# Ten of 25 score blocks: one float32 product a head becomes two float32r products of stacked parts

## The chip, the cores and the metric

The kernel runs on one core of a Trainium2 chip. TensorE (PE in the profile, its weight loads PEld) multiplies, VectorE (DVE), ScalarE (ACT) and GpSimd (POOL) do the elementwise work, and SyncE (SP) issues the DMAs. The metric is the device time of one execution in microseconds (us), as the median of several runs.

## What is computed

A chunked linear recurrence (state-space attention) over 4 batches, 8 heads and 768 steps feeds one layer with a gate. Cut to what matters:

```python
for c in range(nc):                       # chunks of the sequence
    cum = np.cumsum(log_a[chunk])
    L = causal * np.exp(cum[i] - cum[j])
    CB = np.einsum('bhin,bhjn->bhij', Cc, Bc)      # n = 16: this product is changed
    y = einsum(CB * L, xc) + einsum(Cc, state) * np.exp(cum)
    state = decay * state + einsum(Bc * decay_from_j, xc)
h = y @ w_in                              # 3072 x 256 by 256 x 2048
out = (h - tanh(h)) @ w_out               # 2048 x 256
```

All inputs are float32 (the weights arrive as 64-bit floats and are converted in the kernel). Only the product C B^T, with a contraction of 16, is touched.

## The kernel before

The sequence of each batch is cut into 7 chunks of 112 steps (the last has 96): 28 chunks in 14 groups of two. In SBUF each chunk has 128 rows, 16 for the state and 112 for its steps, so that C B^T and C times the state are one product. The eight heads lie as four row groups of 32 partitions (index `i`, 16 of the 32 partitions used) with two heads each (index `w`).

- `load_bc` brings B and C of a group (tile `bc`, three buffers) with four DMAs, one to each row group. `prep` lets POOL write the identity into the state's columns.
- `differences` makes the decay's exponents in bfloat16 (tile `att`, L510). `inner` makes C B^T into the same PSUM tile (L519): for each of 8 heads a float32 product of 16 x 128 weights by up to 116 columns, 16 matmul instructions on PE for the 8 products. `att` has one buffer.
- `weigh` turns `att` into `lt`: exp on ACT (L534), product on DVE (L538), causal mask on POOL (L541). `chunk_y` multiplies `lt` by x (L567) and updates the state (L573). From chunk 10 on, one PE step issues differences and inner of chunk k+1, and then y of chunk k. Such a step is called a chunk block here.
- The layer runs in float32r, a float32 rounded to fewer bits that PE takes in one instruction: operands are split into a high and a low part and three products are summed. `mm1` makes `ph` (L644, 12 matmuls of 256 columns), ACT makes tanh (L659), DVE subtracts (L663, after which the `ph` buffer, one of two, is free), ACT rounds (`gh`, L667), DVE takes the rest (`gl`, L674), and `mm2` makes `o` (L706, 12 matmuls), two steps later. Its sums are taken out by DVE (`pt`, L721, L738) or by ACT and DVE (`ob`).

Each engine works through its own list in order. The lists come from a planner, `Order`: every operation has an engine, a cost that is written in the source and dependencies, and a table `RANK`, one number for each operation, sets the priority. The table was made anew for the change.

Of the kernel before, what the change touches and what calls it, by code (L numbers as in the profile page):

```python
# [9 lines left out]
F32 = mybir.dt.float32  # L10
# [38 lines left out]
MORE = 4  # L49

RANK = """
# [201 lines left out]
def tile_ssm_moe(ctx: ExitStack, tc: tile.TileContext, a, x, bn, bc, wts, out):  # L253
# [30 lines left out]
    def load_bc(G):  # L284


        d = grp[G]
        d["n_bc"] = slot("bc", NGB)

        def fn(i):  # L290
            if i == 0:
                d["bc"] = p2.tile([P, 2, CPG * (P + Q)], F32, tag="bc", name=f"bc{G}", bufs=NGB)
            nc.sync.dma_start(out=d["bc"][32 * i : 32 * i + N], in_=bc[G, i])  # L293

        for i in range(4):
            op("SP", 0.42, lambda i=i: fn(i), w=[d["n_bc"]], dma=KB // 2)
# [36 lines left out]
    cp.tile([P, P - AHEAD], F32, name="behind")  # L333
# [52 lines left out]
    def prep(G):  # L386
# [17 lines left out]
        op("POOL", 0.95, fn_b, r=["wdec", "bi", d["n_b"]], w=[d["n_bw"]])  # L404

# [97 lines left out]
    def need_a(ck):  # L503
        s = ck >= SPAN[0].stop
        return [grp[ck // CPG]["n_bc"], l_c[s], r_c[s]]
# [7 lines left out]
    def inner(ck, more=0):  # L513
        d, at = grp[ck // CPG], CPG * P + ck % CPG * Q
        bb, cc = operands(ck)[0], d["bc"][:, :, at - more : at + qlen(ck)]
        for w in range(2):
            for i in range(4):
                r = slice(32 * i, 32 * i + N)
                nc.tensor.matmul(out=place[1][:, i, 2 + w, N - more : N + qlen(ck)], lhsT=bb[r, w], rhs=cc[r, w],  # L519
                                 start=True, stop=True)  # L520
# [246 lines left out]
    par = cp.tile([P, 2], F32, name="par")  # L767
    ncf = cp.tile([P, N], F32, name="ncf")
# [34 lines left out]
    def consts_dve():  # L803
# [6 lines left out]
        nc.vector.tensor_scalar(out=idn, in0=ncf, scalar1=pidf[:, 1:2], scalar2=None, op0=ALU.is_equal)  # L810

# [26 lines left out]
    op("DVE", 0.9, consts_dve, r=["pid"], w=["idn", "par"])  # L838
# [83 lines left out]
    def plan(g, fn, *args):  # L922
        todo.setdefault(max(g, 0), []).append((fn, args))
# [11 lines left out]
    for ck in at_:  # L935
        if ck <= joint:
            plan(at_[ck][0], chunk_a, ck)
        plan(at_[ck][1], chunk_y, ck, ck >= joint and ck + 1 in at_)
        if (ck + 1) % CPG == 0 and ck // CPG + NGB < NG:
            plan(at_[ck][1], group, ck // CPG + NGB)  # L940
# [59 lines left out]
```

## Time and profile before

| | |
|---|---|
| median of 3 runs | 334.74 us (334.14, 334.74, 337.77) |
| profiled execution | 337.32 us, of which the span is 335.5 us |
| granted clock of TensorE, mean | 0.994 |
| PE, PEld busy | 97%, 93% of the span |
| DVE, ACT, POOL busy | 67%, 57%, 17% of the span |

The span runs from the first to the last instruction; 1.8 us of the profiled execution lie outside. Matmuls overlap on PE, so busy time is not proof of full use; distances from start to start say more. The last ten chunk blocks of the span, at 186.6 to 287 us, are those in which the product is changed.

### The profile page before, as it was taken

How to read it: one execution, taken by the hardware profiler on the slowest of the kernel's cores; microseconds unless marked ns; L12 is line 12 of the kernel's file. 1: busy time of each engine (PE TensorE's matmuls, PEld its weight loads, DVE VectorE, ACT ScalarE, POOL GpSimd, SP SyncE). 2: the span in 40 equal slices, each digit the busy share in tenths (PEclk: the TensorE clock that was granted, in tenths of full speed). 3: DMA queues.
4: the chain of work that ended last, by engine and by line, in shares of the span. 5: the costliest groups of instructions: out<-in, count | busy, mean ns of one | idle time of the engine just before them, and what ended most of it. 6: DMA issues, size and time to landing. Idle time of an engine off the chain costs nothing.

```text
span 335.5 us, 9070 instructions
## 1 busy us (share of the span) xinstructions
PE 325.0 (97%) x3860; PEld 312.8 (93%) x3860; DVE 225.5 (67%) x332; ACT 191.3 (57%) x404; POOL 55.9 (17%) x74
## 2 busy tenths in 40 slices
PE   7979999899999999999999999999999999999995
PEld 6767789899999999999999999999999999999995
DVE  2998999998899966544655655655655655654552
ACT  5866888766565634344655645643655645644441
POOL 6543563310021110000111101101111101100000
PEclk9998999999999999999999999999999999999999
DMA  6959756630011101200211200200200100000000
GB/s 183 243 148 300 230 157 154 202 133 2 3 45 31 47 23 43 64 2 0 63 48 31 64 14 17 64 9 24 63 3 3 33 2 2 31 2 2 31 2 32
DMA packets 12472, 21.41 MB, mean 64 GB/s; under 512 B 2848, under 2 KB 7648, under 8 KB 12432
## 3 DMA queue, kind: packets, MB, share of 16 engines
q1 hardware_dynamic: 12432, 20.84, 21.3%
q8 instruction: 30, 0.49, 0.6%
q14 instruction: 10, 0.08, 0.1%
HBM read 17.51 MB, written 3.32 MB: 62 GB/s over the span
## 4 chain that ended last, share of the span: by engine, by line
PE 86%; DMA 7%; SPq 3%; DVE 2%; issue 1%; POOL 1%; ACT 0%; DVEq 0%
PE o L706 38%; PE ph L644 37%; PE y L567 3%; PE att L519 3%; DMA x<-x_d 2%; DMA raw<-w_d 2%; DMA bc<-bc_d 2%; PE ph L628 2%; DMA braw<-bn_d 1%; SPq L293 1%; PE att L510 1%; PE y L573 1%; PE o L698 1%; POOL lt L541 1%; SPq L324 1%
## 5 line engine op out<-in xcount | busy, mean ns | idle before, releaser
L663 DVE TENSOR_TENSOR g<-ph,g 128x512 f32<-128x512 f32 x96 | 65.9, 690 | 57.9 <-ACT g L659 57.9
L659 ACT ACTIVATE g<-ph 128x512 f32<-128x512 f32 x96 | 57.2, 598 | 74.6 <-PE ph L644 71.4
L644 PE MATMUL ph<-xh,wh 128*128 128x256 f32 x376 | 95.5, 278 | 0.9 <-DVE g L663 0.9
L644 PE MATMUL ph<-xh,wl 128*128 128x256 f32 x376 | 94.9, 277 | 0.0
L674 DVE TENSOR_TENSOR gl<-g,gh 128x512 fp32r<-128x512 f32 x94 | 66.1, 706 | 26.6 <-ACT gh L667 24.2
L667 ACT CAST gh<-g 128x512 fp32r<-128x512 f32 x94 | 58.2, 619 | 36.9 <-DVE g L663 28.8
L644 PE MATMUL ph<-xl,wh 128*128 128x256 f32 x376 | 73.5, 277 | 0.0
L644 PEld LDWEIGHTS ph<-xh,wh 128*128 128x128 f32 x376 | 70.7, 188 | 1.3 <-DVE g L663 1.0
L644 PEld LDWEIGHTS ph<-xh,wl 128*128 128x128 f32 x376 | 70.6, 188 | 0.0
L706 PE MATMUL o<-gh,wh 128*128 128x256 f32 x376 | 60.5, 283 | 0.0
L706 PE MATMUL o<-gh,wl 128*128 128x256 f32 x376 | 58.1, 277 | 0.0
L706 PE MATMUL o<-gl,wh 128*128 128x256 f32 x376 | 58.1, 277 | 0.0
L644 PEld LDWEIGHTS ph<-xl,wh 128*128 128x128 f32 x376 | 56.8, 188 | 0.0
L541 POOL TENSOR_SCALAR_AFFINE_SELECT lt<-lt 128x896 f32<-128x896 f32 (+1 forms) x25 | 28.7, 1148 | 160.9 <-DVE lt L538 145.1
L706 PEld LDWEIGHTS o<-gh,wh 128*128 128x128 f32 x376 | 49.9, 188 | 1.1
L706 PEld LDWEIGHTS o<-gl,wh 128*128 128x128 f32 x376 | 49.8, 188 | 0.0
L706 PEld LDWEIGHTS o<-gh,wl 128*128 128x128 f32 x376 | 49.8, 188 | 0.0
L538 DVE TENSOR_TENSOR lt<-att,lt 128x896 f32<-128x896 f32 (+1 forms) x25 | 26.6, 1065 | 3.4 <-ACT lt L534 2.8
L534 ACT ACTIVATE lt<-att 128x896 f32<-128x896 f32 (+1 forms) x25 | 22.6, 903 | 1.9 <-PE att L519 0.7
L578 ACT COPY x<-y 16x64 f32<-16x64 f32 x96 | 19.4, 202 | 5.4 <-DVE xl L596 3.5
L394 POOL TENSOR_TENSOR bw<-braw,wdec 128x256 f32<-128x256 f32 x14 | 10.3, 746 | 58.2 <-PE y L573 54.4
L567 PE MATMUL y<-lt,x 128*32 128x112 f32 (+1 forms) x448 | 16.3, 263 | 3.1 <-ACT x L578 2.4
(79 smaller groups left out, 258.4 us busy)
## 6 DMA issues: line engine op xcount, KB each, us to landing
raw<-w_d SPq DMA_DIRECT2D x16, 512.0 KB
x<-x_d SPq DMA_DIRECT2D x14, 256.0 KB
bc<-bc_d SPq DMA_DIRECT2D x56, 60.0 KB
out_d<-ob SPq DMA_DIRECT2D x16, 128.0 KB
braw<-bn_d SPq DMA_DIRECT2D x14, 112.0 KB
out_d<-pt SPq DMA_DIRECT2D x8, 128.0 KB
cum<-parts SPq DMA_DIRECT2D x1, 168.0 KB
lt_c<-cum SPq DMA_DIRECT2D x4, 27.0 KB
```

What stands on the lines that cost most here:

```text
L394: nc.gpsimd.tensor_tensor(out=d["b"].rearrange("p c (h n) -> p c h n", h=H), in0=d["braw"].rearrange("p c (h n) -> p c h n", h=H), in1=wd. ...
L534: nc.scalar.activation(k["l"][:, :, 0:q].rearrange("p (i w) q -> p i w q", i=4), place[1][:, :, 0:2, N : N + q], AF.Exp)
L538: nc.vector.tensor_tensor(out=lt, in0=place[1][:, :, 2:4, N : N + q], in1=lt, op=ALU.mult)
L541: nc.gpsimd.affine_select(out=k["l"][:, :, 0:q], in_=k["l"][:, :, 0:q], pattern=[[0, H], [1, q]], compare_op=ALU.is_ge, fill=0.0, base=N, ...
L567: nc.tensor.matmul(out=y[D * h : D * h + D, hg * Q : hg * Q + q], lhsT=d["x"][:, cg, P * hg + D * h : P * hg + D * h + D], rhs=k["l"][:, 4 ...
L578: nc.scalar.copy(grp[(ck + 1) // CPG]["x"][0:N, (ck + 1) % CPG, 2 * D * i : 2 * D * i + 2 * D], k["y"][D * i : D * i + N, H * D : H * D + ...
L644: nc.tensor.matmul(out=ph[:, j, :], lhsT=w_[:, u, 0, k, j * P : (j + 1) * P], rhs=d[("xh", "xl")[p]][:, k, ts], start=p == 0 and k == 0 an ...
L659: nc.scalar.activation(g, gs[t, u][0], AF.Tanh)
L663: nc.vector.tensor_tensor(out=g, in0=ph, in1=g, op=ALU.subtract)
L667: nc.scalar.copy(gh, gs[t, u][1])
L674: on.tensor_tensor(out=gl, in0=g, in1=gh.bitcast(F32), op=ALU.subtract)
L706: nc.tensor.matmul(out=po[t, seg][:, e, :], lhsT=w_[:, u, 1, j, e * P : (e + 1) * P], rhs=g[:, j, :], start=u == seg[0] and k == 0 and j = ...
```

## The change

For groups 9 to 13 (chunks 18 to 27) C B^T is made from float32r parts. B is loaded twice, into both halves of each row group's 32 partitions, and a new step `part_bc` makes from it a tile `bs`: upper half minus the high part of B, lower half its low part, and beside it the high part of C with matching signs. One product with a contraction of 32 then gives high·high + low·high. A second tile, `b2`, holds the low part of C, and a product with a contraction of 16 adds high·low. So 8 float32 products become 16 float32r products, which accumulate in pairs.

```diff
+PARTED = 9
 def load_bc(G):
+    rows, src = (2 * N, bc2[G - PARTED]) if G >= PARTED else (N, bc[G])
-        nc.sync.dma_start(out=d["bc"][32 * i : 32 * i + N], in_=bc[G, i])
+        nc.sync.dma_start(out=d["bc"][32 * i : 32 * i + rows], in_=src[i])
-cp.tile([P, P - AHEAD], F32, name="behind")
+cp.tile([P, P - AHEAD - 40], F32, name="behind")
+def part_bc(G):
+    def fn_h():   # bs: bufs 2
+        nc.scalar.copy(d["bs"][:, :, bb], d["bc"][:, :, bb])
+    def fn_c():
+        nc.scalar.activation(d["bs"][:, :, cc], d["bc"][:, :, cc], AF.Copy, scale=sgn[:, 1:2])
+    def fn_l():
+        nc.vector.scalar_tensor_tensor(out=d["bs"][:, :, bb], in0=d["bc"][:, :, bb], scalar=sgn[:, 0:1],
+                                       in1=d["bs"][:, :, bb].bitcast(F32), op0=ALU.mult, op1=ALU.subtract)
+    def fn_2():
+        nc.vector.scalar_tensor_tensor(out=d["b2"], in0=d["bc"][:, :, wide], scalar=-1.0,
+                                       in1=d["bs"][:, :, wide].bitcast(F32), op0=ALU.mult, op1=ALU.subtract)
+    op("ACT", 0.62, fn_h, ...); op("ACT", 0.55, fn_c, ...); op("DVE", 0.7, fn_l, ...); op("DVE", 0.65, fn_2, ...)
 def inner(ck, more=0):
+    if "bs" in d:
+        for w in range(2):
+            for j in range(2):
+                for i in range(4):
+                    r = slice(32 * i, 32 * i + (2 - j) * N)
+                    rhs = b2[r, w] if j else d["bs"][r, w, at - more : at + qlen(ck)]
+                    nc.tensor.matmul(out=place[1][:, i, 2 + w, N - more : N + qlen(ck)],
+                                     lhsT=d["bs"][r, w, g * P : (g + 1) * P], rhs=rhs, start=j == 0, stop=j == 1)
+        return
...
+        if (ck + 1) % CPG == 0 and PARTED <= ck // CPG + 2 < NG:
+            plan(at_[ck][1], part_bc, ck // CPG + 2)
-    nc = bacc.Bacc("TRN2", target_bir_lowering=False, num_devices=1)
+    nc = bacc.Bacc("TRN2", target_bir_lowering=False, num_devices=1, dynamic_dma_scratch_size=1024)
```

Two small instructions on DVE at the start make the signs `sgn`. The costs that the planner has for PE are as before. The numbers in a tile's name below are those of its chunk or group (`bs9` is of group 9), or of sequence tile and step (`ph6_1`). `x4` are four products of the program.

PE, the chunk block of chunks 18 and 17, the first that is changed. Before:

```order
L644 MATMUL ph6_1_2717<-xl2_2427,wh_84 128x256 x2
L510 LDWEIGHTS lt_c_106
L510 MATMUL att_198<-rt_c_107,lt_c_106 128x2x112
L519 MATMUL att_198<-bc9_1650 128x116 x8
L567 MATMUL y17_2746<-lt17_2645,x8_1519 32x112 x8
```

And of the change, at the same place:

```order
L687 MATMUL ph6_1_2742<-xl2_2027,wh_84 128x256 x2
L543 LDWEIGHTS lt_c_107
L543 MATMUL att_201<-rt_c_108,lt_c_107 128x2x112
L555 MATMUL att_201<-bs9_1748 128x116 x4
L555 MATMUL att_201<-b29_1893,bs9_1748 128x116 x4
L555 MATMUL att_201<-bs9_1748 128x116 x4
L555 MATMUL att_201<-b29_1893,bs9_1748 128x116 x4
L610 MATMUL y17_2780<-lt17_2660,x8_1522 32x112 x8
```

The block stays between the same neighbours; only its middle changes. (The pair of rows for the weights and the matmul of `differences` stands four times in both and is shown once.) Elsewhere on PE one chunk block, of chunks 15 and 14, moves: it stood at 160 us of the profiled span, amid the sequence tile 5, and now stands ahead of `o0_6`, six pieces of the layer after the block at 111 us.

DVE, the busiest place that gets new work, just after the last weights are converted (`wl`, at 111 us before). Before:

```order
L370 TENSOR_TENSOR wl_85<-wv7_1348,wh_84 128x1024
L663 TENSOR_TENSOR g0_6_1745<-ph0_6_1677,g0_6_1745 128x512
L596 TENSOR_TENSOR xl1_806<-y13_1723,xh1_797 128x2x96
L674 TENSOR_TENSOR gl3_4_1782<-g3_4_1598,gh3_4_1671 128x512
L674 TENSOR_TENSOR gl3_5_1786<-g3_5_1692,gh3_5_1742 128x512
L674 TENSOR_TENSOR gl0_6_1803<-g0_6_1745,gh0_6_1784 128x512
L721 TENSOR_TENSOR pt2_986<-o2_4_1695,pt2_986 128x512
L663 TENSOR_TENSOR g0_7_1801<-ph0_7_1768,g0_7_1801 128x512
L538 TENSOR_TENSOR lt14_1765<-att_198,lt14_1765 128x896
```

And of the change:

```order
L373 TENSOR_TENSOR wl_85<-wv7_1351,wh_84 128x1024
L717 TENSOR_TENSOR gl3_4_1767<-g3_4_1601,gh3_4_1674 128x512
L717 TENSOR_TENSOR gl3_5_1771<-g3_5_1695,gh3_5_1745 128x512
L764 TENSOR_TENSOR pt2_989<-o2_4_1698,pt2_989 128x512
L639 TENSOR_TENSOR xl1_809<-y13_1726,xh1_800 128x2x96
L706 TENSOR_TENSOR g0_6_1789<-ph0_6_1680,g0_6_1789 128x512
L581 TENSOR_TENSOR lt14_1769<-att_201,lt14_1769 128x896
L706 TENSOR_TENSOR g0_7_1805<-ph0_7_1773,g0_7_1805 128x512
L717 TENSOR_TENSOR gl0_6_1826<-g0_6_1789,gh0_6_1809 128x512
L425 SCALAR_TENSOR_TENSOR bs9_1748<-bc9_1653,sgn_95,bs9_1748 128x2x256
```

`g0_6` moves behind two `gl`, a `pt` and `xl`, and the first of the new operations follows four rows later. 

SP, the loads of the last groups. Before, `bc10` follows the four stores of `pt`, and `bc11` to `bc13` come one by one, each beside its `x`. Of the change:

```order
L296 DMA bc10_1913<-bc2_d 32x960 x4
L791 DMA out_d<-pt0_568 128x256 x2
L791 DMA out_d<-pt1_906 128x256 x2
L791 DMA out_d<-pt2_989 128x256 x2
L791 DMA out_d<-pt3_1174 128x256 x2
L791 DMA out_d<-ob4_2426 128x256 x2
L308 DMA x10_2518<-x_d 128x512
L317 DMA braw1_101<-bn_d 112x256
L296 DMA bc11_2653<-bc2_d 32x960 x4
L296 DMA bc12_2678<-bc2_d 32x960 x4
L296 DMA bc13_2703<-bc2_d 32x960 x4
```

`bc10` now stands ahead of the stores, and the last three groups follow each other, each with twice the partitions (32 for 16).

More of the change, by code (lines that the diff above doesn't have):

```diff
@@ L252, in tile_ssm_moe @@
 @with_exitstack
-def tile_ssm_moe(ctx: ExitStack, tc: tile.TileContext, a, x, bn, bc, wts, out):
+def tile_ssm_moe(ctx: ExitStack, tc: tile.TileContext, a, x, bn, bc, bc2, wts, out):
     nc = tc.nc
@@ L292, in fn @@
                 d["bc"] = p2.tile([P, 2, CPG * (P + Q)], F32, tag="bc", name=f"bc{G}", bufs=NGB)
-            nc.sync.dma_start(out=d["bc"][32 * i : 32 * i + N], in_=bc[G, i])
+            nc.sync.dma_start(out=d["bc"][32 * i : 32 * i + rows], in_=src[i])
         for i in range(4):
-            op("SP", 0.42, lambda i=i: fn(i), w=[d["n_bc"]], dma=KB // 2)
+            op("SP", 0.42, lambda i=i: fn(i), w=[d["n_bc"]], dma=KB // 2 * rows // N)
     def load_x(G):
@@ L404, in prep @@
         op("POOL", 0.95, fn_b, r=["wdec", "bi", d["n_b"]], w=[d["n_bw"]])
+    def part_bc(G):
+        d = grp[G]
+        if G < PARTED:
+            return
+        d["n_bs"], d["n_b2"] = slot("bs", 2), slot("b2", 2)
+        bb, cc = slice(0, CPG * P), slice(CPG * P, CPG * (P + Q))
+        def fn_h():
+            d["bs"] = p2.tile([P, 2, CPG * (P + Q)], F32R, tag="bs", name=f"bs{G}")
+            nc.scalar.copy(d["bs"][:, :, bb], d["bc"][:, :, bb])
[5 more added lines that the diff above has]
+        def fn_2():
+            d["b2"] = p2.tile([P, 2, 8 + CPG * Q], F32R, tag="b2", name=f"b2{G}")
+            wide = slice(CPG * P - 8, CPG * (P + Q))
+            nc.vector.scalar_tensor_tensor(out=d["b2"], in0=d["bc"][:, :, wide], scalar=-1.0,
+                                           in1=d["bs"][:, :, wide].bitcast(F32), op0=ALU.mult, op1=ALU.subtract)
+        op("ACT", 0.62, fn_h, r=[d["n_bc"]], w=[d["n_bs"]])
+        op("ACT", 0.55, fn_c, r=[d["n_bc"], "sgn"], w=[d["n_bs"]])
+        op("DVE", 0.7, fn_l, r=[d["n_bc"], "sgn"], w=[d["n_bs"]])
+        op("DVE", 0.65, fn_2, r=[d["n_bc"], d["n_bs"]], w=[d["n_b2"]])
     def qlen(ck):
@@ L503, in need_a @@
     def need_a(ck):
-        s = ck >= SPAN[0].stop
-        return [grp[ck // CPG]["n_bc"], l_c[s], r_c[s]]
+        s, d = ck >= SPAN[0].stop, grp[ck // CPG]
+        return [*([d["n_bs"], d["n_b2"]] if "n_bs" in d else [d["n_bc"]]), l_c[s], r_c[s]]
     def differences(ck):
@@ L513, in inner @@
     def inner(ck, more=0):
-        d, at = grp[ck // CPG], CPG * P + ck % CPG * Q
+        d, at, g = grp[ck // CPG], CPG * P + ck % CPG * Q, ck % CPG
+        if "bs" in d:
+            b2 = d["b2"][:, :, 8 + g * Q - more : 8 + g * Q + qlen(ck)]
+            for w in range(2):
[3 more added lines that the diff above has]
+                        rhs = b2[r, w] if j else d["bs"][r, w, at - more : at + qlen(ck)]
+                        nc.tensor.matmul(out=place[1][:, i, 2 + w, N - more : N + qlen(ck)], lhsT=d["bs"][r, w, g * P : (g + 1) * P],
+                                         rhs=rhs, start=j == 0, stop=j == 1)
+            return
         bb, cc = operands(ck)[0], d["bc"][:, :, at - more : at + qlen(ck)]
@@ L767, in tile_ssm_moe @@
     par = cp.tile([P, 2], F32, name="par")
+    sgn = cp.tile([P, 2], F32, name="sgn")
     ncf = cp.tile([P, N], F32, name="ncf")
@@ L810, in consts_dve @@
         nc.vector.tensor_scalar(out=idn, in0=ncf, scalar1=pidf[:, 1:2], scalar2=None, op0=ALU.is_equal)
+        nc.vector.tensor_scalar(out=sgn[:, 0:1], in0=pidf[:, 1:2], scalar1=float(N), scalar2=None, op0=ALU.is_ge)
+        nc.vector.tensor_scalar(out=sgn[:, 1:2], in0=sgn[:, 0:1], scalar1=2.0, scalar2=-1.0, op0=ALU.mult, op1=ALU.add)
     def table(i):
@@ L837, in tile_ssm_moe @@
     op("ACT", 0.61, lambda: nc.scalar.activation(la.rearrange("p h (b c) -> p c b h", b=NB), a_sb, AF.Ln), r=["a", "tab"], w=["la"])
-    op("DVE", 0.9, consts_dve, r=["pid"], w=["idn", "par"])
+    op("DVE", 0.9, consts_dve, r=["pid"], w=["idn", "par", "sgn"])
     op("ACT", 1.4, lambda: table(1), r=["la"], w=["tab"])
@@ L979 @@
     w_out = np.asarray(moe_w_out).view(np.uint64).reshape(NCONV, 2, P, DM).transpose(2, 0, 1, 3).reshape(P, NCONV, 512)
+    bc = np.ascontiguousarray(np.concatenate([heads(B, N), heads(C, 0)], axis=4))
     ins = {
@@ L984 @@
         "bn_d": rows(lay(B, 0, Q)),
-        "bc_d": np.ascontiguousarray(np.concatenate([heads(B, N), heads(C, 0)], axis=4)),
+        "bc_d": bc[:PARTED],
+        "bc2_d": np.ascontiguousarray(np.concatenate([bc[PARTED:]] * 2, axis=2)),
         "w_d": np.ascontiguousarray(np.stack([w_in, w_out], axis=2)),
     }
-    nc = bacc.Bacc("TRN2", target_bir_lowering=False, num_devices=1)
+    nc = bacc.Bacc("TRN2", target_bir_lowering=False, num_devices=1, dynamic_dma_scratch_size=1024)
     args = []
```

91 rows, old and new, of the table RANK are left out of this document.

## The prediction

> **What bounds the kernel now.** I read the page's first part, then a table by stages, then the chain that ended last, and then single rows in the order of time where the change falls.
>
> ```profile
> PE 325.0 (97%) x3860; PEld 312.8 (93%) x3860; DVE 225.5 (67%) x332; ACT 191.3 (57%) x404; POOL 55.9 (17%) x74
> ```
>
> ```profile
> core 0: us, PE busy (x) PEld busy (x) DVE busy (x) ACT busy (x) POOL busy (x), PEclk, DMA share, GB/s
> 96.00:160.00 64.00, 64.00 (x683) 63.27 (x682) 43.95 (x63) 31.39 (x59) 6.23 (x6) 1.00 0.11 33
> 185.00:290.00 105.00, 105.00 (x1316) 102.14 (x1315) 60.91 (x90) 57.80 (x123) 11.40 (x15) 1.00 0.08 24
> ```
>
> PE is never empty in the stretch that holds all ten changed blocks (185 to 290 us), nor in the one where new work for DVE and ACT begins; DVE is busy 58% and 69% of the two, ACT 55% and 49%. So the end is set by how fast PE gets through its list. The chain says the same, and gives the prices of the pieces around a chunk block:
>
> ```profile
> 94.56 1.41 PE ph L644 x12
> 95.98 0.21 PE att L510 x4
> 96.18 0.45 PE att L519 x16
> 96.64 0.52 PE y L567 x16
> 97.16 0.12 PE y L573 x16
> 97.28 1.57 PE o L706 x12
> 98.85 1.36 PE ph L644 x12
> ```
>
> Only the row of L519 is changed. What it holds PE for is read from start to start, in the order of time (the first number is the start, the second the length up to the end of the last one):
>
> ```profile
> 160.31 0.29 PE L519 MATMUL att<-bc 16*128 16x116 f32 x4
> ...
> 160.31 0.62 PE L519 MATMUL att<-bc 16*128 16x116 f32 x16
> 160.87 0.59 PE L567 MATMUL y<-lt,x 128*32 128x112 f32 x16
> ...
> 211.35 0.62 PE L519 MATMUL att<-bc 16*128 16x100 f32 x16
> 211.91 0.59 PE L567 MATMUL y<-lt,x 128*32 128x112 f32 x16
> ...
> 111.81 0.54 PE L567 MATMUL y<-lt,x 128*32 128x96 f32 x16
> ```
>
> From the first product to y are 0.56 us. All ten blocks together hold PE for 10 x 0.56 = 5.6 us, which caps any gain: 1.7% of the time.
>
> **What sets the 0.56 us** decides everything. The 16 matmuls of a block come in four rounds of four, one for each row group: the first four lie in 0.29 us, hardly more than the 0.27 us of one.
>
> ```profile
> L519 PE MATMUL att<-bc 16*128 16x116 f32 x224 | 8.7, 271 | 0.0
> L519 PEld LDWEIGHTS att<-bc 16*128 16x128 f32 x400 | 13.5, 187 | 0.0
> L567 PEld LDWEIGHTS y<-lt,x 128*32 128x32 f32 x448 | 9.7, 109 | 6.9 <-issue 2.2 <-POOL lt L473 1.0 <-POOL lt L541 1.0
> L644 PEld LDWEIGHTS ph<-xh,wh 128*128 128x128 f32 x376 | 70.7, 188 | 1.3 <-DVE g L663 1.0
> L510 PEld LDWEIGHTS <-lt_c 9*128 9x128 bf16 x100 | 2.6, 90 | 3.7 <-issue 0.7 <-DVE g L663 0.3
> ```
>
> The last start is 0.62 - 0.27 = 0.35 us behind the first; less the 0.02 us within a round, three steps take 0.33 to 0.34 us, **0.11 us a round**. Two things could take that long: streaming the columns, or loading the next weights. If it were the columns, a block of 100 columns would be shorter than one of 116 by 14%, 0.05 us. It isn't: the rows at 160.31 and 211.35 both say 0.62, and y follows both after 0.56. Where columns do set the pace it shows: y with 112 columns lasts 0.59, with 96 columns 0.54. What the two blocks share is the weight load of 128 columns. Its length grows from 109 ns for 32 columns to 187 ns for 128, 0.81 ns a column, or 104 ns for 128 without the fixed part: about a round. I read the block as **bound by its weight loads**, with the stream of columns hidden behind them.
>
> **The change part by part.**
>
> 1. *The products.* Removed: 16 matmul instructions with 16 weight loads a block; added: 16 with 16 weight loads, again 128 columns each, in rounds of four row groups. The stream of a product shrinks, the loads don't. Is a float32r load as long? Its rows (L644) say 188 ns, against 187 ns; only bfloat16 is shorter (90 ns). And in the layer, a float32r matmul of 256 columns comes every 1.36/12 = 0.113 us (98.85 in the chain), so a 128-column float32r load fits into 0.113 us. Four rounds of 0.11 us stay four rounds of 0.11 us: **0**. The rest of the block, 0.56 - 0.35 = 0.21 us until y starts, is the same for 116 and 100 columns, so a shorter last stream shouldn't shorten it either. Bounds of an operation that the trace doesn't have (float32r on 116 columns): if everything followed the stream, the block would halve, -0.28 us, times ten -2.8 us; if a new product cost as much as an old one, it would double, +5.6 us. I take the row that lies nearest, the block of 100 columns, with a stream shortened by 14% and nothing gained, and allow 0.01 us a block: **-0.1 us**.
>
> The Trainium skill, "TensorE: Matmul & The Clock Gate", section "LDWEIGHTS (loading the stationary operand)", has a rule that speaks against the change: a load takes its columns divided by 1.2 GHz, whatever the contraction, which is 107 ns here. By it a round can't fall under 0.107 us, and ten blocks could gain some 10 x 4 x 0.004 = 0.2 us at most; the rounds of this trace agree with it.
>
> 2. *The parts.* ACT gets a cast of 512 and a scaled copy of 448 columns, DVE two operations of 512 and 464, for each of five groups.
>
> ```profile
> L667 ACT CAST gh<-g 128x512 fp32r<-128x512 f32 x94 | 58.2, 619 | 36.9 <-DVE g L663 28.8 <-PE o L706 8.0
> L363 DVE SCALAR_TENSOR_TENSOR wv<-wv,wm 128x512 uint32<-128x512 uint32 x2 | 1.4, 686 | 0.0
> ...
> L359 DVE SCALAR_TENSOR_TENSOR wm<-wv,wm 128x512 uint32<-128x512 uint32 x2 | 1.7, 830 | 0.0
> ```
>
> At 0.62 us and 0.56 us on ACT and 0.69 to 0.83 us each on DVE, a group costs 1.2 us and 1.4 to 1.6 us. Both have room: DVE has 20 us free in the first stretch above for two groups and 44 us in the second for three, ACT more. What hides it is the slack of the chain from `ph` to its release:
>
> ```profile
> 186.17 0.39 PE L644 MATMUL ph<-xl,wh 128*128 128x256 f32 x2
> ...
> 186.65 0.60 ACT L659 ACTIVATE g<-ph 128x512 f32<-128x512 f32 x1 [0.74 <-PE ph L644]
> ...
> 187.28 0.69 DVE L663 TENSOR_TENSOR g<-ph,g 128x512 f32<-128x512 f32 x1 [0.65 <-ACT g L659]
> ```
>
> `ph` is done at 186.56 and freed at 187.97, 1.4 us later. With two buffers PE wants it back three pieces of 1.36 us after its end, 4.1 us: 2.7 us of slack, against 1.6 us of new work at most in one place. At the densest spot, after the last `wl`, I went through the new list by hand with these lengths.
>
> ```profile
> 110.84 1.22 DVE L370 TENSOR_TENSOR wl<-wv,wh 128x1024 fp32r<-128x1024 f32 x1
> ...
> 113.42 0.62 PE L706 MATMUL o<-gl,wh 128*128 128x256 f32 x4
> ```
>
> `wl` ends at 112.0, two `gl` take it to 113.4, `pt` must wait for the end of `o2_4` (114.0), then `pt`, `xl` and `g0_6` end at 114.7, 115.1 and 115.7. PE wants that `ph` buffer at 116.7, two pieces after `o2_4`. Nothing is late: **0**. Without that cover the price would be the excess itself, up to 1.6 us once.
>
> 3. *The loads.* Twice the bytes for five groups, on queues that are 8 to 11% busy: 0. The one new wait with something behind it is on ACT: the cast of `bs10` stands between two tanh, and its load waits for the block of chunk 15, now at 121 us. The rows of before:
>
> ```profile
> 161.00 2.75 SPq L293 DMA_DIRECT2D bc<-bc_d  x4
> ...
> 165.63 0.24 POOL L401 COPY bc<-idn 128x64 f32<-128x64 f32 x1 [1.46 <-DMA bc<-bc_d]
> ...
> 124.32 0.84 SPq L748 DMA_DIRECT2D out_d<-pt  x2
> ```
>
> From issue to use were 4.9 us, so from 121.5 it is ready at 126.4, and 1 to 2 us later if twice the bytes take twice the flight. ACT comes to it at about 127.1: from 114.0 PE needs five pieces (120.8), the block (1.3), `o0_6` (1.57 + 1.36) and one more piece, 126.4, and a tanh. On SP the stores stand behind this load; they were issued at 124.3 and come no later, and no one waits for them. At worst ACT stands for 1.3 us with tanh and `gh` behind it, inside the 2.7 us. **0**, else up to 1.5 us.
>
> 4. *The moved block, the start, the memory.* A chunk block has the same pieces at 121 us as at 160 us, and PE is full at both: 0. The two small operations at the start stand ahead of a DVE operation that waits for its weights; even uncovered they are 0.3 us. Tiles behind the changed padding move by some bytes; nothing in the trace prices that, see the third rival.
>
> The sum: span 335.5 - 0.1, or 337.2 us for the profiled execution of 337.32. That execution stands 2.6 us above the median of 334.74, so in the median I expect **334.6 us**, no change. About 1% is what a measurement of this kernel can tell from none.
>
> **The rivals.**
>
> *The stream sets the round.* Two products of one pass replace one that streams twice in each of two instructions, and the block halves: -2.8 us, 331.9 us. For it speaks that a float32 matmul of 256 columns takes twice a float32r one:
>
> ```profile
> 31.20 1.99 PE L698 MATMUL o<-g,wv 128*128 128x256 f32 x8
> ```
>
> (1.99/8 = 0.25 against 0.113 us.) Against it speak the blocks of 100 columns. The Trainium skill, "FP8 and Floating Point Precision", section "TensorE Precision Notes", gives true float32 four passes and the reduced form one truncated read, which would halve the ten streams; by that rule alone the sum is this rival's, and the two rows of L519 stand against it.
>
> *The short product is slow* (the other side). The trace has float32r only with 256 columns. If on 116 columns it ran at the pace of float32, each of the 16 products would cost what one of the 8 does now: the block doubles, +5.6 us, 340.3 us. It is slower than before as soon as a new product costs more than half an old one, and by 1% from 0.8 of it. Against it: where columns set the pace in this trace (y), the time falls with them and shows no floor.
>
> *The layer's matmuls change their pace.* Up to the block at 96 us they take 1.41 us for 12 (0.118 us each), after it 1.36 (0.113 us), with the same clock of 1.00; a block was where it changed. If changed blocks or moved tiles put them back to 0.118 us, the 800 or so of 185 to 290 us (1316 less ten blocks of 52) lose 0.0046 us each: +3.7 us, 338.3 us. Against it: y, behind the changed part, is as before.
>
> *A late part.* One of the waits in 2 or 3 isn't covered: +0.5 to 2 us, some 336 us.
>
> **How the numbers follow.** No change: 0.70. The stream sets the round: 0.12. A slow short product: 0.05. A changed pace: 0.06. A late part: 0.07. The forecast with the late part holds 0.77, so the range also takes in the halved block: 331.8 to 336.5 us; the forecast's own is 334.1 to 335.1 us. Faster by over 1% needs more than the halved block (0.84%), so 0.05; slower by over 1% are the second and third rival, 0.10; within 1% remain 0.85.
>
> **What would show it.** In the new profile: the changed line as two groups of 80 matmuls (contraction 32 and 16), weight loads of some 187 ns, and a length of a block, from its first product to y, of 0.56 us (0.28 for the first rival, over 1 for the second); 1.36 us for 12 matmuls of the layer around them; no wait of PE longer than 0.1 us behind 96 us. The forecast is wrong if the load of float32r weights into a row group of 32 is shorter than I read it, since then 0.56 us isn't a floor.

## The result, and the profile after

The change made the kernel slower by 1%: 339.54 us (median of 337.14, 338.75, 340.34 and 340.88) against 335.19 us for the kernel before (four runs, the three from above among them), a ratio of 1.0102 with an interval of 1.0053 to 1.0152. The forecast of 334.6 us and its range up to 336.5 us were missed. The profiled execution happened to be the quickest of the four: 337.14 us, a span of 335.4 us.

The page's first part and the table by stages, as shown of before:

```profile
PE 325.8 (97%) x3860; PEld 314.3 (94%) x3860; DVE 232.4 (69%) x344; ACT 196.8 (59%) x414; POOL 57.2 (17%) x74
```

```profile
core 0: us, PE busy (x) PEld busy (x) DVE busy (x) ACT busy (x) POOL busy (x), PEclk, DMA share, GB/s
96.00:160.00 64.00, 64.00 (x679) 63.14 (x678) 45.49 (x67) 32.55 (x61) 6.72 (x7) 1.00 0.13 41
185.00:290.00 105.00, 105.00 (x1282) 102.74 (x1267) 64.52 (x96) 60.63 (x131) 12.03 (x13) 1.00 0.06 19
```

PE still has no gap in either stretch, at a granted clock of 1.00, and the other engines have nearly as much room as before (DVE is busy 64.5 of 105 us, where it was 60.9). PE waits for none of them; its own list takes longer. The chain of work that ended last shows where (start, length, piece). First a chunk block at 92.5 us in which the product isn't changed, then one in which it is:

```profile
91.11 1.36 PE ph L687 x12
92.47 0.21 PE att L543 x4
92.68 0.45 PE att L562 x16
93.13 0.52 PE y L610 x16
93.65 0.12 PE y L616 x16
93.77 1.61 PE o L749 x12
95.38 1.41 PE ph L687 x12
...
219.58 1.36 PE ph L687 x12
220.94 0.21 PE att L543 x4
221.15 0.41 PE att L555 x16
221.56 0.47 PE y L610 x16
222.02 0.12 PE y L616 x16
222.14 1.61 PE o L749 x12
223.75 1.41 PE ph L687 x12
225.16 1.41 PE o L749 x12
```

The changed products are even quicker by 0.04 us (`att` L555 0.41, where L519 had 0.45). But behind either block 12 matmuls of the layer, the same instructions on the same tiles, take 1.41 us in place of 1.36. The durations of one line in two stretches between blocks (minimum, median, maximum in ns) say it for each matmul:

```profile
L749 PE MATMUL o<-gh,wl x16: 276/276/277, 198.0 to 206.5; 128*128 128x256 f32 x16
...
L749 PE MATMUL o<-gh,wl x12: 281/281/281, 225.5 to 231.5; 128*128 128x256 f32 x12
```

Counted from start to start, a layer matmul comes every 113.3 ns or every 117.8 ns. The pace is one or the other for a whole stretch between two chunk blocks; it changes only where a block lies between. Behind the first of the two blocks above (it ends at 94 us here and at 97 us in the profile of before; called the block at 94 us from here on) there are 17 such stretches with 1860 layer matmuls. Before, all 17 run at 113.3 ns, in the profile shown and in a second one. After, 9 of them with 888 matmuls run at 117.8 ns: 888 x 4.5 ns = **4.0 us**. Against it stand 0.05 us for each of ten changed blocks. From the first layer matmul behind the block at 94 us to the end of the span the change takes 241.7 us, and before took 238.3 us: +3.4, where 4.0 - 0.5 makes 3.5.

That both profiled executions have a span of some 335.5 us is chance: the kernel before came out of that block at 97.2 us, the changed one at 93.7 us. A second profile of before came out at 93.8 us. Some 1.5 us of the 3.5 are the pace again: ahead of the block, 324 layer matmuls ran at 117.8 ns in the first profile of before and at 113.3 ns in that of the change.

### The profile page after: what moved, and what is told of

The parts are those of the page before. It is cut to its first block, busy times and chain, and to the rows that moved or that the text cites. A ratio compares the mean times of both kernels' runs of the same rounds, so it can differ in the third digit from the quotient of the medians.

```text
span 335.4 us, 9097 instructions
## 1 busy us (share of the span) xinstructions
PE 325.8 (97%) x3860; PEld 314.3 (94%) x3860; DVE 232.4 (69%) x344; ACT 196.8 (59%) x414; POOL 57.2 (17%) x74
## 2 busy tenths in 40 slices
DMA packets 12792, 22.64 MB, mean 67 GB/s; under 512 B 2848, under 2 KB 7648, under 8 KB 12752
## 4 chain that ended last, share of the span: by engine, by line
PE 81%; DMA 10%; DVE 4%; SPq 2%; issue 1%; ACT 0%; POOL 0%; POOLq 0%; DVEq 0%
PE o L749 38%; PE ph L687 36%; DMA raw<-w_d 5%; DMA bc<-bc_d 4%; PE y L610 3%; DMA braw<-bn_d 1%; PE att L555 1%; SPq L296 1%; PE att L543 1%; PE att L562 1%; DVE wv L366 1%; DVE lt L501 1%; PE y L616 1%; DVE rt_c L527 1%; DVE wl L373 1%
## 5 line engine op out<-in xcount | busy, mean ns | idle before, releaser
L749 PE MATMUL o<-gh,wh 128*128 128x256 f32 x376 | 60.9, 284 | 0.0
L584 POOL TENSOR_SCALAR_AFFINE_SELECT lt<-lt 128x896 f32<-128x896 f32 (+1 forms) x25 | 29.5, 1181 | 121.3 <-DVE lt L581 104.5
L397 POOL TENSOR_TENSOR bw<-braw,wdec 128x256 f32<-128x256 f32 x14 | 12.0, 868 | 96.7 <-PE y L616 92.7
```

What stands on the lines that cost most here:

```text
L397: nc.gpsimd.tensor_tensor(out=d["b"].rearrange("p c (h n) -> p c h n", h=H), in0=d["braw"].rearrange("p c (h n) -> p c h n", h=H), in1=wd. ...
L584: nc.gpsimd.affine_select(out=k["l"][:, :, 0:q], in_=k["l"][:, :, 0:q], pattern=[[0, H], [1, q]], compare_op=ALU.is_ge, fill=0.0, base=N, ...
L749: nc.tensor.matmul(out=po[t, seg][:, e, :], lhsT=w_[:, u, 1, j, e * P : (e + 1) * P], rhs=g[:, j, :], start=u == seg[0] and k == 0 and j = ...
```

## The experiments

The table holds all of them, with this sum for each: what it took in its profile from the first layer matmul behind the block at 94 us to the end of the span, and how many of the 1860 layer matmuls were in stretches at 117.8 ns. The experiments were run in four sessions on different chips; each ratio is to the kernel before in the same session, so ratios compare across rows better than medians do.

| kernel | median, us | ratio to before (95%) | 94 us block to end, us | matmuls at 117.8 ns |
|---|---|---|---|---|
| before, first profile | 334.74 | | 238.3 | 0 |
| e1, before again | 335.29 | 1.0001 (0.9965 to 1.0038) | 238.3 | 0 |
| changed | 339.54 | 1.0102 (1.0053 to 1.0152) | 241.7 | 888 |
| e2, changed again | 340.63 | 1.0134 (1.0058 to 1.0210) | 243.9 | 1392 |
| e3, before, weights moved | 335.54 | 1.0011 (0.9981 to 1.0040) | 238.2 | 0 |
| e4, changed, weights back | 341.40 | 1.0125 (1.0030 to 1.0219) | 243.9 | 1392 |
| e5, before, block tiles -128 | 338.93 | 1.0107 (1.0030 to 1.0185) | 240.9 | 624 |
| e6, changed, block tiles back | **334.10** | **0.9943 (0.9907 to 0.9979)** | 237.9 | 0 |
| e7, order alone | 339.04 | 1.0081 (1.0052 to 1.0110) | 242.0 | 888 |
| e8, order and parts | 339.14 | 1.0080 (1.0047 to 1.0114) | 242.4 | 972 |
| e9, before, lt_c and rt_c -128 | 334.48 | 0.9966 (0.9928 to 1.0004) | 238.2 | 0 |
| e10, before, bc -128 | 335.54 | 1.0006 (0.9970 to 1.0041) | 238.2 | 0 |
| e11, before, x -128 | 340.39 | 1.0134 (1.0100 to 1.0169) | 241.0 | 624 |
| e12, before, bw -128 | 340.07 | 1.0137 (1.0091 to 1.0183) | 243.7 | 1236 |
| e13, before, x, bw, lt -128 | 340.48 | 1.0122 (1.0074 to 1.0170) | 243.6 | 1236 |
| e14, before, x, bw -256 | 334.92 | 0.9986 (0.9953 to 1.0019) | 238.2 | 0 |
| e15, changed, x, bw back | 335.74 | 0.9991 (0.9956 to 1.0027) | 238.8 | 192 |
| e16, changed, half the weights | 333.55 | 0.9916 (0.9879 to 0.9953) | 237.6 | 360 |

With the old products the fourth column is 238.3 plus 4.5 ns for each matmul of the fifth, to 0.3 us in every row; with the new ones (changed, e2, e4, e6, e15) it is some 0.4 to 0.7 us less than that.

**Is the pace drawn anew, or does the kernel fix it?** In the expectations of the first four runs, theory 1 is that the place of tiles in SBUF decides the pace, the converted weights wh and wl above all; theory 2 that the changed program does (its work, its order or its products); theory 3 that it is drawn anew in each build or execution. e1 and e2 are the two kernels unchanged.

> The unchanged kernel, for a second profile of it. In its first profile every run of layer matmuls behind 97 us came at 113.3 ns a matmul; only two earlier ones came at 117.8 ns. Theory 1 (the place of the converted weights in memory sets how often the slow pace occurs): again all fast behind 97 us, about 335 us. Theory 2 (the new work or the moved block disturbs the pace): the same. Theory 3 (the pace is drawn anew in each execution, and the first profile was a lucky one): about half of the runs of layer matmuls behind 97 us are at 117.8 ns in this profile too.

> The changed kernel, for a second profile of it. In its first profile 9 of 18 runs of layer matmuls behind 93 us came at 117.8 ns. Theories 1 and 2: a similar share again, 337 to 341 us. Theory 3: any share, as in a second profile of the kernel before.

Before is at 113.3 ns again behind the block at 61 us, and the changed kernel again has more than half of its 17 stretches (the text above counts 18) at 117.8 ns, if not the same ones. So the kernel decides whether the slower pace occurs there, and theory 3 falls. What does differ between two profiles of one kernel is the pace ahead of the block at 94 us: 117.8 and 113.3 ns in those of before, 113.3 and 117.8 ns in those of the change. In both profiles of the changed kernel the pace goes back and forth from block to block between 94 and 180 us already, ahead of the first new product (184 us). The new products can't be what sets it off.

**The converted weights.** The change moves every tile in SBUF: the scratch for DMAs shrinks by 15 x 1024 bytes, `sgn` adds 32 bytes, the padding `behind` loses 160. e3 puts wh and wl of the kernel before where the change has them (1280 in place of 256, modulo 4096 bytes) and holds all other tiles modulo 4096; e4 puts them back to 256 in the changed kernel, and lt to gl to their old addresses.

```diff
 # e3, in before
-    cp.tile([P, P - AHEAD], F32, name="behind")
+    cp.tile([P, P - AHEAD + 2816], F32, name="behind")
-    nc = bacc.Bacc("TRN2", target_bir_lowering=False, num_devices=1)
+    nc = bacc.Bacc("TRN2", target_bir_lowering=False, num_devices=1, dynamic_dma_scratch_size=1024)
 # e4, in the changed kernel
-    cp.tile([P, P - AHEAD - 40], F32, name="behind")
+    cp.tile([P, P - AHEAD - 40 + 256], F32, name="behind")
-    nc = bacc.Bacc("TRN2", target_bir_lowering=False, num_devices=1, dynamic_dma_scratch_size=1024)
+    nc = bacc.Bacc("TRN2", target_bir_lowering=False, num_devices=1, dynamic_dma_scratch_size=4096)
```

> The kernel before with nothing changed but the place of its tiles: the smaller scratch space of the change moves the converted weights by 15360 bytes (their place modulo 4096 goes from 256 to 1280, as in the change), and the padding behind them is widened so that the layer's other operands keep their place modulo 4096. Theory 1 (place): slow as the change, some 1% over before, with about half of the runs of layer matmuls behind 97 us at 117.8 ns. Theory 2 (new work): as before, all at 113.3 ns. Theory 3 (drawn anew): no difference from before in the median.

> The changed kernel with its tiles put back: scratch space of 4096 bytes and 1024 bytes more padding, so that the converted weights lie as before modulo 4096 (256) and the operands of the layer at the very addresses of before. All work and its order are those of the change. Theory 1 (place): all runs of layer matmuls behind 97 us at 113.3 ns, and the time at or 0.5 us under before's (a block is 0.05 us shorter in the change's profile). Theory 2 (new work): stays 1% over before. Theory 3: no difference from the change in the median.

Neither moved the time, and e4 has the 1392 slow matmuls of e2 in the same stretches. The place of the weights is not it, though the layer's matmuls read them.

**The chunk blocks' tiles, the new work, or the new order.** Both e3 and e4 left one thing: -160 + 32 = -128 bytes, modulo 1024, for the tiles behind the padding up to `lt`. Of these PE reads `lt_c`, `rt_c`, `bc`, `x` and `bw` behind 94 us. e5 does that to the kernel before, e6 takes it back in the changed one. In each a spare tile ahead of `lt` keeps `lt` to `gl` where they were; e7 has one of 2848 floats in place of `bs` and `b2`.

```diff
 # e5, in before
-    cp.tile([P, P - AHEAD], F32, name="behind")
+    cp.tile([P, P - AHEAD - 32], F32, name="behind")
+    pp.tile([P, 32], F32, name="pad")
 # e6, in the changed kernel
-    cp.tile([P, P - AHEAD - 40], F32, name="behind")
+    cp.tile([P, P - AHEAD - 8], F32, name="behind")
+    pp.tile([P, 992], F32, name="pad")
 # e7 and e8, in the changed kernel: the old products in all blocks
-        if "bs" in d:
+        if False:
-        return [*([d["n_bs"], d["n_b2"]] if "n_bs" in d else [d["n_bc"]]), l_c[s], r_c[s]]
+        return [*([d["n_bs"], d["n_b2"], d["n_bc"]] if "n_bs" in d else [d["n_bc"]]), l_c[s], r_c[s]]
 # e7 besides: nothing is made in part_bc
+        fn_h = fn_c = fn_l = fn_2 = lambda: None
```

> The kernel before with only the chunk blocks' own tiles moved: x, bc, bw, lt_c and rt_c lie 128 bytes lower, as they do modulo 1024 in the changed kernel; everything else has its old address. Theory A (the place of the chunk blocks' tiles decides whether the layer's matmuls leave a block at 113 or at 118 ns): about half of the runs between blocks at 118 ns, +3 to +4.5 us, 338 to 340 us. Theory B (the new work on ACT and DVE decides it) and theory C (the new order decides it): all at 113 ns behind 97 us, 335.1 us, no change.

> The changed kernel with the chunk blocks' tiles put back to their place modulo 1024 bytes of before, lt to gl at their old addresses. Theory A: all runs behind 97 us at 113 ns, and the shorter blocks show, 334.6 us (0.5 us under the kernel before). Theories B and C: still alternating, 338.5 to 341 us.

> The changed kernel's order, loads and places, with the four operations of part_bc left out and the old float32 products in all blocks. Theory B (the new work on ACT and DVE): 113 ns throughout, about 335 us. Theories A (places) and C (order): alternating from block to block, 338.5 to 340.5 us. If the shorter new blocks were the cause instead: 335 us as well.

> As the one before it (old float32 products, the changed kernel's order and places), but with the four operations of part_bc made, so that only the products differ from the changed kernel. Theory B (new work): alternating, 338.5 to 341 us. Theories A and C: alternating too. Only if the new products are what turns the pace: 113 ns throughout, about 335 us.

Theory A, the place, explains all four. The kernel before, with nothing but its block tiles 128 bytes lower, turns 1% slower (e5). The changed kernel with them put back is at 113.3 ns in all 17 stretches and beats both: 334.1 us, 0.57% under before (0.21 to 0.93%). Its profile accounts for a part of this only: behind the block at 94 us it takes 0.4 us less than before, near the 0.5 us that ten shorter blocks make. Where the rest of the 0.57% (some 1.9 us) lies isn't shown. e7 and e8 alternate with the old products, without and with the new work, so neither the parts nor the products are needed for the loss. The order's own part isn't told apart by them, as they have the moved tiles too; but e6 has the new order and all the new work, and shows no loss. Its chain, at the same two blocks of chunks:

```profile
207.79 1.36 PE ph L689 x12
...
210.39 1.58 PE o L751 x12
211.97 2.72 PE ph L689 x24
...
220.13 1.36 PE ph L689 x12
221.49 0.21 PE att L545 x4
221.70 0.40 PE att L557 x16
222.10 0.47 PE y L612 x16
222.57 0.12 PE y L618 x16
222.69 1.57 PE o L751 x12
224.26 1.36 PE ph L689 x12
```

1.36 us on both sides of the blocks, and 0.40 us for the new products.

**Which tile.** From e3's base, where the tiles of the blocks lie as before, one tile at a time goes 128 bytes lower, between two spare tiles of 992 and 32 floats that leave all else in place modulo 4096 bytes (the weights modulo 1024). The cut shows e11.

```diff
+                p2.tile([P, 992], F32, tag="pad992", name="pad992", bufs=1)
             d["x"] = p2.tile([P, CPG, H * D], F32, tag="x", name=f"x{G}", bufs=NGB)
+                p2.tile([P, 32], F32, tag="pad32", name="pad32", bufs=1)
```

> The kernel before, with lt_c and rt_c alone (both operands of the four difference products, which a chunk block begins with) 128 bytes lower; all else keeps its place modulo 4096 bytes, the converted weights modulo 1024. If this is the tile that counts: the layer's runs alternate between 113 and 118 ns, 338.5 to 339.5 us. If not: all at 113 ns behind 97 us, 335.2 us. I hold it for the least likely of the four: the pace is chosen at the exit of a block, and these products are its entrance.

> The same with bc alone 128 bytes lower (both operands of the products att). If it counts: alternating, about 339 us; if not, 335.2 us. The changed kernel reads bs and b2 there in its last ten blocks and alternates in them as before, which speaks against it.

> The same with x alone 128 bytes lower (the weights of the 16 long y products, and the streamed operand of the 16 short ones that end a block). If it counts: alternating, about 339 us; if not, 335.2 us. With bw the likeliest: the last matmul of a block reads it.

> The same with bw alone 128 bytes lower (the weights of the 16 short products that end a block). If it counts: alternating, about 339 us; if not, 335.2 us. If none of the four alternates, it is not the place of one tile but how two of them lie to each other, or a tile that TensorE does not read.

The operands of the differences and of C B^T don't count; `x` alone and `bw` alone each turn the kernel 1.3% slower. These are the two operands of the 16 short products with which a chunk block ends. The chain of e12 shows the rule of its stretches, back and forth at every block:

```profile
197.21 1.41 PE ph L648 x12
...
199.92 1.57 PE o L710 x12
201.50 1.36 PE ph L648 x12
...
209.66 1.36 PE ph L648 x12
...
212.30 1.61 PE o L710 x12
213.91 2.83 PE ph L648 x24
...
222.39 1.41 PE ph L648 x12
...
225.05 1.57 PE o L710 x12
226.62 1.36 PE ph L648 x12
```

A stretch at 1.41 us is followed by one at 1.36 and the other way round, at each of the 17 blocks. The last of these, at 301 us, holds the 32 products of `y` alone, no differences and no C B^T, and the pace changes there too (1.36 us ahead of it, 1.41 us behind). In the kernel before a block is left at 113.3 ns whichever pace led into it: the one at 94 us was entered at 117.8 ns in its first profile, at 113.3 ns in its second. How much an execution loses depends on which of the two sets of stretches is hit: 624 matmuls in e5 and e11, 1236 in e12 and e13, where the same blocks alternate from the other end. Which set it is follows from the pace ahead of the block at 94 us: 117.8 ns in the profiles of e5 and e11, 113.3 ns in those of e12 and e13.

**Places to each other, or of their own; the period; the cure.** e13 lowers `x`, `bw` and `lt` together, e14 lowers `x` and `bw` by 256 bytes, e15 puts only `x` and `bw` (and `wv` between them) back in the changed kernel, each with spare tiles as above. e16 is for the other step of the prediction: e6 with only 64 of the 128 weight columns in the new products.

```diff
 # e16, on e6
-   nc.tensor.matmul(out=place[1][:, i, 2 + w, N - more : N + qlen(ck)], lhsT=d["bs"][r, w, g * P : (g + 1) * P],
+   nc.tensor.matmul(out=place[1][0:64, i, 2 + w, N - more : N + qlen(ck)], lhsT=d["bs"][r, w, g * P : g * P + 64],
```

> The kernel before with x, bw and lt all 128 bytes lower, so that the operands of the y products keep their places to each other. Theory R (what counts is how x lies to bw and to lt): all runs at 113 ns behind 97 us, 335.2 us. Theory S (x and bw each have a place of their own that counts): alternating between 113 and 118 ns, 339 to 340.5 us.

> The kernel before with x and bw 256 bytes lower. If places count modulo 256 bytes: all at 113 ns, 335.2 us. If modulo 512 or more: alternating, 339 to 340.5 us. I lean to the second, since x is read in lines of 128 bytes, four to a round, one for each group of columns.

> The changed kernel with x and bw (and wv between them, which TensorE reads in the first 60 us) put back to their places modulo 1024 bytes of before; bc, lt_c and rt_c stay where the change has put them. If x and bw are all that counts: 113 ns behind 97 us and the shorter blocks, 334 to 334.8 us. If the place of another tile or the new products matter too: alternating, 338.5 to 341 us.

> The changed kernel with all the chunk blocks' tiles put back (the one at 113 ns throughout), and in the last ten chunks the products take only 64 of the 128 weight columns, so that half of the decayed scores of these chunks is left out; the streamed columns are as many. If the weight load sets the rounds: the later rounds fall from 111 ns to what the stream of 116 columns needs, an estimate of 50 to 70 ns from the 113 ns of 256 columns; a block loses about 0.2 us and the kernel about 2 us, 332 us. If the stream or a fixed time a round sets them: rounds of 111 ns, 334 us.

e13 alternates, so it is not how `x` and `bw` lie to each other and to `lt`; each has a place that counts (theory S). The layer's operands kept their places modulo 256 bytes in all experiments, so a place relative to them isn't excluded. e14 doesn't alternate, against my leaning: 256 bytes lower is as good as before. Modulo 256 bytes both tiles start at 192 in the kernel before and at 64 in the changed one. Of the starts tried, 192 is good and 64 is bad, for each of the two. Within a tile the pieces of the heads follow each other, 128 bytes each in `x` and 64 in `bw`, so with either start some products read at 192 and others at 64; a move by 128 bytes changes which product reads at which place modulo 256, and one by 256 bytes doesn't. The Trainium skill, "SBUF — State Buffer", section "Specifications (TRN2)", gives cache lines of 16 bytes, and a penalty for each cross to a new one; a move by 128 bytes changes nothing by that rule, so the +1.3% of e11 and e12 is not in it.

e15 takes the loss back: its time is that of before (0.9991), and of the stretches at 117.8 ns two of 17 remain in its profile, 192 matmuls or 0.9 us. Both lie behind new products. e6, which also puts `bc`, `lt_c` and `rt_c` back, has none. Whether one of these matters beside the new products, or chance does, one profile each doesn't say.

In e16 the groups and a piece of the chain show what half the weight columns do:

```profile
L557 PEld LDWEIGHTS att<-bs 32*64 32x64 f32 x80 | 2.9, 134 | 0.0
```

```profile
220.88 0.21 PE att L545 x4
221.09 0.23 PE att L557 x16
221.32 0.47 PE y L612 x16
221.79 0.12 PE y L618 x16
221.90 1.61 PE o L751 x12
```

The loads fall from 186 to 134 ns and the products from 0.40 to 0.23 us, with as many columns streamed. From start to start the later rounds fall from 111 to 58 ns, and the way from the last product to y from 200 to 146 ns. From the first product to y a block falls from 0.57 to 0.40 us, 1.7 us for ten. The two blocks with 100 columns have later rounds of 58 to 59 ns as well, so the stream doesn't set them even with half the weights. Yet from the block at 94 us to the end e16 takes only 0.3 us less than e6 (237.6 against 237.9): in its profile 360 matmuls are at 117.8 ns, so 1.6 us are given back by the pace, and the 332 us that were expected became 333.55. With places that are good for e6, a shorter block can still be left at the slower pace.

## Why the prediction was wrong

*The bound.* Right: PE waits for nothing from 97 us to 328 us in any of the profiles, and what the kernel gained or lost was the length of PE's list.

*1, the products.* Right in its mechanism. The block stayed bound by its weight loads:

```profile
220.91 0.31 PE L555 MATMUL att<-bs 32*128 32x116 f32 x4
221.05 0.28 PE L555 MATMUL att<-b,bs 16*128 16x116 f32 x4
221.16 0.28 PE L555 MATMUL att<-bs 32*128 32x116 f32 x4
221.27 0.28 PE L555 MATMUL att<-b,bs 16*128 16x116 f32 x4
221.49 0.54 PE L610 MATMUL y<-lt,x 128*32 128x96 f32 x16
```

Rounds of 0.11 us (0.14 for the first), and 0.57 us to y where 0.56 were forecast, though a float32r instruction takes half as long for its columns as a float32 one (0.113 against 0.22 us from start to start for 256 columns, L644 and L698 of before). e16 shows the bound: with half the weight columns the rounds take half the time, whether 100 or 116 columns are streamed. (Half the weight columns are half the rows of the result too; these two aren't told apart.) The Trainium skill, "TensorE: Matmul & The Clock Gate", section "LDWEIGHTS (loading the stationary operand)", whose rule was weighed there, makes 107 ns of 128 columns and 53 ns of 64; the rounds measured 111 and 58. One small term was missing from the sum: the first product now starts 28 ns after the differences, where it was 96 (83 in the blocks with 100 columns). So a block became shorter by 0.05 us and the ten by 0.5 us, not by 0.1. The rivals of a stream that sets the round, and of a slow short product, are out.

*2, the parts.* Right.

```profile
L425 DVE SCALAR_TENSOR_TENSOR bs<-bc,sgn,bs 128x512 fp32r<-128x512 f32 x5 | 4.2, 834 | 0.1
L422 ACT ACTIVATE bs<-bc,sgn 128x448 fp32r<-128x448 f32 x5 | 3.4, 672 | 0.0
L431 DVE SCALAR_TENSOR_TENSOR b<-bc,bs 128x464 fp32r<-128x464 f32 x5 | 3.2, 634 | 0.1
L419 ACT CAST bs<-bc 128x512 fp32r<-128x512 f32 x5 | 3.1, 614 | 0.0
```

1.29 us on ACT and 1.47 on DVE a group (about 1.2 and 1.4 to 1.6 were forecast), and PE doesn't wait for them.

*3, the loads, and the moved block.* Right: no wait of PE there, and e6 has both without a loss.

*4, the memory.* **This is the step that failed**: "Tiles behind the changed padding move by some bytes; nothing in the trace prices that", booked at 0 with a chance of 0.06 for the third rival, which is what happened. Its price was near, 3.7 us against 4.0, but by luck, since other matmuls paid it: I charged all of the 800 from 185 to 290 us, and it was half of 1860 from 94 us on. Moved tiles did it, as that rival allowed, and changed blocks were not needed. What the trace of before held, and I gave too little weight: the same matmuls at two paces with the same clock, in one execution, with the switch at a chunk block. A pace with two states that no engine, queue or clock explains is a term of the sum, with a weight like that of an unknown, not a remark in a rival. That `y` behind the changed part is as before was no argument against it, since the operands that decide the pace, `x` and `bw`, are read behind the changed part, at the block's end.

## What to carry to other kernels

Where the same matmuls run at two paces in one trace, find out what switches them before any change is priced: here 128 bytes in the place of one small operand cost 1.3% (e11, e12), more than twice what the changed kernel gains with good places (0.57%, of which its ten shorter blocks explain 0.15%). A change that moves memory is two changes; run it once more with the old places, modulo a power of two, before it is judged. And small products that share the array in rounds cost their weight columns: fewer passes or a shorter stream brought little here (rounds of 111 ns either way), and half the weight columns brought rounds of 58 ns.

## What the runs showed of the hardware

- Back-to-back float32r matmuls of 128 x 128 weights and 256 columns come every 113.3 ns or every 117.8 ns, with a granted clock of 1.00 in both. The pace changed only across a chunk block, where small products in row and column groups stand between the whole ones, and held until the next, for up to 420 matmuls in e12.
- Which pace follows depends on where the operands of the last small products lie: with `x` and `bw` starting at 192 bytes modulo 256, the block at 94 us and every later one with the old products is left at 113.3 ns, in six profiles; with either starting at 64 it is left at the pace that it wasn't entered with. Earlier blocks, whose PE still waits for others now and then, don't keep to this.
- Behind blocks of the new products neither rule holds. With the bad places the changed kernel keeps 113.3 ns across three of them in a row; with the good ones two of ten (e15) and four of ten (e16) are left at 117.8 ns. Chance alone it isn't: from the third of these blocks on, three profiles of the new products with bad places (changed, e2, e4) have the same paces, though they enter the block at 94 us at different ones.
- Open are the cause inside the engine, which use of `x` counts (it is streamed in the last 16 products, and is the weights of the 16 before), places other than 64 and 192, and what decides the pace behind the new products.
